# A tuned attention and gated-FFN kernel: the first gate ahead of the sixth pair's outputs, and the attention pieces of one stage a position on

## The chip, the cores and the metric

The kernel runs on one core of a Trainium2 chip. The metric is device time in microseconds of one execution. The engines are TensorE (PE, with its weight loads shown as PEld), VectorE (DVE), ScalarE (ACT), GpSimd (POOL) and SyncE (SP), which issues the DMAs.

## The reference

Sliding-window attention, then a gated FFN on its output, in float32:

```python
scores = scale * np.matmul(q, k.transpose(0, 1, 3, 2))      # 8 batches, 8 heads, 576 x 64
mask = (rel >= 0) & (rel < window)                           # window 64
scores = np.where(mask, scores, -1000000000.0)
scores = scores - np.max(scores, axis=-1, keepdims=True)
attn = np.exp(scores)
attn = attn / (np.sum(attn, axis=-1, keepdims=True) + 1e-09)
x = np.matmul(attn, v)                                       # then laid out as 4608 tokens x 512
gate = 1.0 / (1.0 + np.exp(-(x @ w_gate)))                   # w_gate, w_val: 512 x 1536
val = x @ w_val
return (gate * val @ w_out).astype(np.float32)               # w_out: 1536 x 512
```

The weights come as float64 and are made into float32 on the chip.

## The kernel before, in words

**Tiles.** The 4608 tokens are cut into 12 tiles t of 384. A tile's attention is done in four head pairs p. The suffix of a name tells both: p0_4_0 is head 0 of pair 0 of tile 4. The FFN runs over 12 hidden blocks j of 128. To keep float32 accuracy, each operand of a large product is split into a high and a low part (the names x, w, hh and hl), and each product is three matmuls.

**A head pair's attention** goes through stages. `scores` (L208) is 24 small matmuls into s. `exponentials` masks and takes a row minimum on VectorE (L232), then exps on ScalarE (L241), with row sums rs. `invert` (L249, L250) makes quotients of the sums, and `normalize` (L259) multiplies them in, on VectorE for tiles 4 and 5, on GpSimd for tiles 0 to 2. `stage_b` transposes on TensorE (L290, tile pp) and copies to pT on ScalarE (L295). `stage_c` or `outputs` multiplies with v on TensorE (L319, tile oo), and x (L325 on ScalarE, L326 on VectorE) is the split result.

**The FFN of tiles 0 and 1** is plain. `up_gate` and `up_val` are twelve matmuls each into ph0 and ph1 (L349). The gate is a sigmoid on ScalarE (L372), h32 and its split follow on VectorE (L394, L386, L388), and the down product is y (L419). Exp and sigmoid need different function tables on ScalarE, and a change between them shows as ACT_TABLE_LOAD. The weight conversion of each block (L111 and L112, L145 on ScalarE; L120, L122, L124, L146 on VectorE) runs beside it.

**Tiles 2 to 11** go in five pairs s = 1 to 5, by a scheme of seven products in place of eight. For each k of 0 to 5, products n = 0 to 6 are made for the gate (m = 0) and then for the value (m = 1), in `product` (L568, tile pr). VectorE adds them up: p1, u1, u3, c3, c5, c6 (L574, L580). Gates come behind products 3 to 6 of m = 0. One product of one m is a slot: 14 to a k, 84 to an s. During s the attention of the next two tiles is done between the products; for s = 1 these are tiles 4 and 5. Weight sums for s = 1 are built on GpSimd (L496 to L499) and split into ws, by a cast on ScalarE (L145) and a subtraction on GpSimd (L146).

**The order.** Each piece of work is put into a list with a time and a priority:

```python
def put(tm, o, f, *a):
    events.append((tm, o, f, a))
```

The list is sorted, and each engine gets its instructions in that order, moved a little by a scheduler. So the numbers in the calls of `put` say only the order. For the attention of the first two tiles, n = 0 to 7 counts the eight pairs, with times 3.6 apart and an offset for each stage. The first `up_gate` and `up_val` of tile 0 are put from `now` on. For the pair stages, a dictionary `fill` says which stage is issued behind which slot: number 3 is `stage_s` (scores and exps, with the outputs of the pair before), 4 `stage_n` (quotients), 1 `stage_b` (transposes and copies), 2 `stage_c`.

Of the kernel before, what the change touches and what calls it, by code (L numbers as in the profile page):

```python
# [26 lines left out]
def attn_ffn(ctx: ExitStack, tc: tile.TileContext, qT, kT, vN, w_gate, w_val, w_out, out):  # L27
# [31 lines left out]
    for h in range(2):  # L59
        rows = band[h * BLK:(h + 1) * BLK]  # L60
        nc.gpsimd.affine_select(out=rows, in_=rows, pattern=[[1, P]], compare_op=ALU.is_ge,
                                fill=NEG, base=-1, channel_multiplier=-1)
        nc.gpsimd.affine_select(out=rows, in_=rows, pattern=[[-1, P]], compare_op=ALU.is_ge,
                                fill=NEG, base=BLK, channel_multiplier=1)
    for h, key in enumerate(((1, 0), (0, 1))):
# [3 lines left out]
                                fill=NEG, base=-BLK, channel_multiplier=0)  # L69
# [545 lines left out]
    def hidden_b(s, j):  # L615
        r, k = divmod(j, NK)
        hidden_split(2 * s + 1, j, hb[(s, k)][:, r, :], nc.vector)
# [5 lines left out]
    def put(tm, o, f, *a):  # L623
        events.append((tm, o, f, a))
# [16 lines left out]
    for n in range(2 * NP):  # L641
        t, p = divmod(n, NP)
        for f, d in zip((scores, softmax, stage_b, stage_c),
                        (0, 3.5 if n > 1 else 0, {6: 9.2, 7: 7.3}.get(n, 10.6), {6: 10.4}.get(n, 12.2))):
            put(A0 + 3.6 * n + d, 6, f, t, p)


# [1 line left out]
    def unit(s, n):  # L649
        return 2 * s + n // 2 % 2, n // 4 + n % 2 * 2  # L650

    plan, fill = [], {}
# [7 lines left out]
    at, now = {}, 0.0  # L660
# [5 lines left out]
    def attend(i):  # L666
        nonlocal now
        for f, t, p, *done in fill.get(i, ()):
            if f in (0, 3):
                put(now - LOAD_AHEAD, 8, load_qk, t, p)  # L670
                put(now - LOAD_AHEAD, 8.5, load_v, t, p)
            put(now, 6, stages[f], t, p, *done)
            now += APT[f]

    for i, (kind, t, j) in enumerate(plan):
        attend(i)
        at[(kind, t, j)] = now
        if (kind, t, j) == ("up", 0, 0):
            now = -9
        if kind == "up":  # L680
            put(now, 9, up_gate, t, j)
            now += UPT / 2
            attend(i + 0.5)
            put(now, 9, up_val, t, j)
            if t == 1 and j < NF - KEEP:
                put(now, 9.1, put_hidden, t, j)
            now += UPT / 2
        else:
            for x in range(TB):
                put(now + x * DPT, 9, down, t, j, x, j == 0, j == NF - 1)  # L690
            now += DNT
        if (kind, t, j) == ("up", 0, 0):
            now = 0.0
# [11 lines left out]
    def last_tile(t, js, ready):  # L705


        nonlocal now
        items = [(j, x) for x in range(TB) for j in js[:2]] + [(j, x) for j in js[2:-2] for x in range(TB)]
        items += [(j, x) for x in range(TB) for j in js[-2:]]  # L710
        for n, j in enumerate(js):
            put(now + n * DNT - ready[0], 9.4, ready[1], t, j)
        for n, (j, x) in enumerate(items):
            if n % TB == 0 and t == 1:
                attend(len(plan) + n // TB)
                attend(len(plan) + n // TB + 0.5)
            put(now, 9, down, t, j, x, j == js[0], j == js[-1])
            now += DPT
# [6 lines left out]
    for s in range(1, NS):  # L725
        a, b = 2 * s, 2 * s + 1
        for c in range(2):
            put(now - 21 + 10 * c, 5, x_parts, s, c)
            for n in range(NPR):
                put(now - 19.5 + 10 * c + 1.2 * n, 5.5, x_part, s, n, c)  # L730
                put(now - 18 + 10 * c + 1.2 * n, 5.6, x_rest, s, n, c)
        downs = []
        fill.clear()
        if s + 1 < NS:

            for n, (i, d) in enumerate(((2, 7), (12, 9), (26, 5), (33, 9), (47, 5), (54, 9), (68, 5), (75, 5))):
                fill[i] = [(3, *unit(s + 1, n), *([unit(s + 1, n - 1)] if n else []))]
                fill[i + (2 if n else 4)] = [(4, *unit(s + 1, n))]
                fill[i + d] = [(1, *unit(s + 1, n))]
            fill[82] = [(2, *unit(s + 1, n))]  # L740
        slot = 0
        for k in range(NK):
            if s == 1:
                for m in range(2):
                    for d, f in ((-6, sums_load), (0, sums_make), (7, sums_split), (11, sums_store)):
                        put(now - (21 if k else 38) + 13 * m + d, 7, f, m, k)
                for x, d in enumerate((-18, -14, -5)):
                    put(now + d, 7.5, a_load, s, k, x)
            else:
                for q in range(NPR):  # L750
                    put(now - 24 + 3 * q, 7.5, w_load, s, k, q)
            for m in range(2):
                for n in range(NPR):
                    put(now, 9, product, s, k, m, n)
                    now += PRT
                    if n in (2, 4, 6) and len(downs) > (RESERVE if m else 0) * (k == 1):
                        j, x = downs.pop(0)
                        put(now, 9, down, a, j, x, j == 0, False)
                        now += DPT
                    attend(slot)  # L760
                    slot += 1
            downs += [(j, x) for j in (k, k + NK) for x in range(TB)]
        for j, x in downs:
            put(now, 9, down, a, j, x, False, j == NF - 1)
            now += DPT
        last_tile(b, [n // 2 + (n % 2) * NK for n in range(NF)],
                        (4, lambda t, j, s=s: hidden_b(s, j)))
# [59 lines left out]
```

## Time and profile before

| what | value |
|---|---|
| time, median of 3 runs | 1007.4 us (1005.68 to 1008.06) |
| time of the profiled execution | 1007.45 us |
| its span | 1005.6 us |
| TensorE busy | 978.7 us (97%) |
| VectorE, ScalarE, GpSimd busy | 642.6, 530.7, 232.1 us |
| granted TensorE clock, mean | 0.996 of full |

The span runs from the first to the last instruction that the profiler saw; the time of the run is 1.85 us longer. Busy times are sums over all instructions of an engine. TensorE's weight loads lie beside its matmuls and are counted apart.

### The profile page before, as it was taken

Reading aid. Unit: us, or ns where it says so; the run is one execution under the profiler, and the core shown is the slowest. Engines: PE = TensorE matmul, PEld = TensorE weight load, DVE = VectorE, ACT = ScalarE, POOL = GpSimd, SP = SyncE. Lnnn points to the kernel's source line nnn. Section 1 sums busy time; section 2 is a strip of 40 time slices with the busy share of each in tenths; the row PEclk is TensorE's granted clock in tenths of the full one; section 3 lists DMA queues with packets and bytes.
Section 4 is the critical chain, followed back from the end, with each engine's and each line's share of the span. In section 5 each row is a group of like instructions: output and inputs, shape, how many; then the busy total and the mean of one; then the engine's idle time right before and its main releaser. Section 6 shows DMA issues by size and latency. Waiting matters only on the chain.

```text
span 1005.6 us, 19700 instructions
## 1 busy us (share of the span) xinstructions
PE 978.7 (97%) x6984; PEld 882.5 (88%) x6984; DVE 642.6 (64%) x1737; ACT 530.7 (53%) x1433; POOL 232.1 (23%) x240
## 2 busy tenths in 40 slices
PE   6899999999999999999999999999999999999998
PEld 4788999888888888999988999988999998999996
DVE  7799888636666664666665666565666667344532
ACT  7888887635645745545554554464565464211122
POOL 4210113226453130212131121213211124010100
PEclk9999999999999999999999999999999999999999
DMA  9999988478875624766642676661776652466500
GB/s 298 333 323 361 340 280 273 159 237 291 262 253 195 213 90 166 243 211 222 213 152 86 231 247 199 221 193 42 239 229 218 208 183 72 157 213 206 189 32 32
DMA packets 115057, 208.91 MB, mean 208 GB/s; under 512 B 9360, under 2 KB 61840, under 8 KB 114960
## 3 DMA queue, kind: packets, MB, share of 16 engines
q1 hardware_dynamic: 114960, 207.66, 63.0%
q8 instruction: 56, 0.92, 0.4%
q14 instruction: 41, 0.34, 0.1%
HBM read 165.94 MB, written 41.68 MB: 206 GB/s over the span
## 4 chain that ended last, share of the span: by engine, by line
PE 64%; ACT 4%; DVE 1%; issue 0%; DVEq 0%; ACTq 0%
PE pr L568 35%; PE y L419 23%; PE s L208 2%; ACT p L241 2%; PE pp L290 2%; PE s L319 1%; ACT g L362 1%; ACT e L361 0%; PE pr L319 0%; PE oo L319 0%; DVE u L574 0%; ACT L241 0%; DVE rs L249 0%; DVE c L574 0%; DVE g L366 0%
## 5 line engine op out<-in xcount | busy, mean ns | idle before, releaser
L419 PE MATMUL y<-w,hh 128*128 128x512 f32 x804 | 250.2, 392 | 0.0
L568 PE MATMUL pr<-x_T,wt 128*128 128x384 f32 x1152 | 226.3, 338 | 0.4
L568 PEld LDWEIGHTS pr<-x_T,wt 128*128 128x128 f32 x1152 | 202.2, 188 | 10.9 <-DVE u L574 4.1
L568 PE MATMUL pr<-x_B,wt 128*128 128x384 f32 x864 | 176.4, 340 | 0.1
L419 PEld LDWEIGHTS y<-w,hh 128*128 128x128 f32 x804 | 148.3, 188 | 21.3 <-ACT hh L384 1.3
L419 PE MATMUL y<-w,hl 128*128 128x512 f32 x402 | 158.2, 394 | 0.0
L568 PEld LDWEIGHTS pr<-x_B,wt 128*128 128x128 f32 x864 | 150.5, 188 | 8.2 <-issue 2.6
L574 DVE TENSOR_TENSOR u<-pr,p 128x384 f32<-128x384 f32 x120 | 66.5, 554 | 137.1 <-PE pr L568 136.7
L259 POOL TENSOR_TENSOR p<-p,rs 128x384 f32<-128x384 f32 x76 | 65.8, 880 | 291.1 <-DVE rs L250 212.0
L241 ACT ACTIVATE p<-p,mn 128x128 f32<-128x128 f32 x288 | 111.1, 394 | 23.0 <-DVE mn L232 22.2
L388 POOL TENSOR_TENSOR hl<-h,hh 128x384 fp32r<-128x384 f32 x48 | 49.8, 1039 | 283.4 <-DVE hh L386 283.4
L349 PE MATMUL ph<-x,w 128*128 128x384 f32 x576 | 106.8, 339 | 0.0
L349 PEld LDWEIGHTS ph<-x,w 128*128 128x128 f32 x576 | 100.1, 189 | 2.0 <-issue 1.0
L419 PEld LDWEIGHTS y<-w,hl 128*128 128x128 f32 x402 | 75.3, 187 | 17.8 <-DVE hl L388 1.6
L232 DVE CUSTOM_DVE_ANT_0 p<-s,m 128x128 f32<-128x128 f32 x288 | 66.2, 286 | 14.8 <-PE s L208 14.8
L574 DVE TENSOR_TENSOR c<-pr,u 128x384 f32<-128x384 f32 x120 | 66.7, 555 | 9.9 <-ACT g L372 4.8
L388 DVE TENSOR_TENSOR hl<-hb,hh 128x384 fp32r<-128x384 f32 x60 | 39.1, 663 | 41.1 <-ACT hh L384 40.7
L295 ACT COPY pT<-pp 128x384 f32<-128x384 f32 x96 | 41.7, 482 | 42.9 <-PE pp L290 42.4
L582 ACT COPY p<-pr 128x384 f32<-128x384 f32 x48 | 22.5, 470 | 68.1 <-PE pr L568 67.8
L384 ACT CAST hh<-hb 128x384 fp32r<-128x384 f32 x60 | 30.0, 513 | 51.2 <-PE y L419 51.2
L208 PE MATMUL s<-k,q 64*64 64x128 f32 x1152 | 45.9, 288 | 8.9 <-DMA k<-in_kT_dram 6.9
L574 DVE TENSOR_TENSOR c<-pr,p 128x384 f32<-128x384 f32 x60 | 33.4, 557 | 27.9 <-PE pr L568 27.0
(95 smaller groups left out, 1409.6 us busy)
## 6 DMA issues: line engine op xcount, KB each, us to landing
wt<-wd SPq DMA_DIRECT2D x168, 512.0 KB, 4.0
v<-in_vN_dram SPq DMA_DIRECT2D x48, 384.0 KB, 4.7
wd<-ws SPq DMA_DIRECT2D x48, 256.0 KB, 3.6
k<-in_kT_dram SPq DMA_DIRECT2D x48, 224.0 KB, 4.8
q<-in_qT_dram SPq DMA_DIRECT2D x48, 192.0 KB, 4.6
wd<-w SPq DMA_DIRECT2D x36, 256.0 KB, 5.8
wa<-wd SPq DMA_DIRECT2D x36, 256.0 KB, 4.0
out_dram<-yo SPq DMA_DIRECT2D x33, 256.0 KB, 2.0
```

The costliest lines, as they stand in the source:

```text
L208: pe(nc.tensor.matmul(sc[h][half * BLK:(half + 1) * BLK, u, :], qt[h * BLK:(h + 1) * BLK, U * BLK:(U + 1) * BLK], kt[h * BLK:(h + 1) * BLK ...
L232: nc.vector.tensor_tensor_reduce(out=pt[:, u, :], in0=sc[:, u, :], in1=masks[key], op0=ALU.add, op1=ALU.min, scale=-SCALE, scalar=3.0e38, ...
L241: exp = nc.scalar.activation(pt[:, u, :], pt[:, u, :], AF.Exp, bias=mn[:, u:u + 1], scale=-1.0, **sums)
L259: eng.tensor_mul(out=pt, in0=pt, in1=rs.unsqueeze(2).broadcast_to([P, UP, P]))
L295: cp = nc.scalar.copy(pT, pp)
L349: pe(nc.tensor.matmul(ph, l, r, start=i == 0, stop=i == len(prs) - 1))
L384: nc.scalar.copy(h_hi, h32)
L388: return eng.tensor_sub(out=h_lo, in0=h32, in1=h_hi.bitcast(F32))
L419: pe(nc.tensor.matmul(yb[y], l, r, start=first and n == 0, stop=last and n == 2))
L568: pe(nc.tensor.matmul(ps, l, r, start=new and i == 0, stop=i == len(prs) - 1, skip_group_check=not new))
L574: nc.vector.tensor_add(out=o, in0=ps, in1=a)
L582: nc.scalar.copy(tmp["p1"], ps)
```

## The change

It has two parts. In the head, the transposes of the eighth pair (n = 7) are due one unit earlier, the outputs of the seventh (n = 6) two units later, and the first gate starts at -9.9 in place of -9. In stage s = 1 alone, the scores of the first pair move from slot 2 to slot 5, all quotients go three slots behind their scores (they went two behind, the first four), and the transposes of five of the eight pairs go six slots behind their scores; four of these went five behind before, and the first pair's go from slot 9 to slot 11.

```diff
--- before.py
+++ after.py
@@ -641,7 +641,7 @@
     for n in range(2 * NP):
         t, p = divmod(n, NP)
         for f, d in zip((scores, softmax, stage_b, stage_c),
-                        (0, 3.5 if n > 1 else 0, {6: 9.2, 7: 7.3}.get(n, 10.6), {6: 10.4}.get(n, 12.2))):
+                        (0, 3.5 if n > 1 else 0, {6: 9.2, 7: 6.3}.get(n, 10.6), 12.4 if n == 6 else 12.2)):
             put(A0 + 3.6 * n + d, 6, f, t, p)
 
 
@@ -676,7 +676,7 @@
         attend(i)
         at[(kind, t, j)] = now
         if (kind, t, j) == ("up", 0, 0):
-            now = -9
+            now = -9.9
         if kind == "up":
             put(now, 9, up_gate, t, j)
             now += UPT / 2
@@ -733,9 +733,13 @@
         fill.clear()
         if s + 1 < NS:
 
-            for n, (i, d) in enumerate(((2, 7), (12, 9), (26, 5), (33, 9), (47, 5), (54, 9), (68, 5), (75, 5))):
+
+            slots = ((2, 7), (12, 9), (26, 5), (33, 9), (47, 5), (54, 9), (68, 5), (75, 5))
+            if s == 1:
+                slots = ((5, 6), (12, 9), (26, 6), (33, 9), (47, 6), (54, 9), (68, 6), (75, 6))
+            for n, (i, d) in enumerate(slots):
                 fill[i] = [(3, *unit(s + 1, n), *([unit(s + 1, n - 1)] if n else []))]
-                fill[i + (2 if n else 4)] = [(4, *unit(s + 1, n))]
+                fill[i + (3 if s == 1 else 2 if n else 4)] = [(4, *unit(s + 1, n))]
                 fill[i + d] = [(1, *unit(s + 1, n))]
             fill[82] = [(2, *unit(s + 1, n))]
         slot = 0
```

TensorE in the head, from the transposes of pair 1_1 (pp) to the first gate product of tile 1 (ph0_1_0), before (repeated rows of a group left out):

```order
L290 MATMUL pp1_1_1_686<-ident_105,p1_1_1_566 128x128 x3
L319 MATMUL oo_1_1_716<-pT0_1_1_684,v_1_1_216 64x64
...
L290 MATMUL pp0_1_2_732<-ident_105,p0_1_2_626 128x128 x3
...
L349 MATMUL ph0_0_0_744<-x_0_0_388,w0_0_447 128x384 x3
...
L319 MATMUL oo_1_2_759<-pT0_1_2_736,v_1_2_224 64x64
...
L290 MATMUL pp0_1_3_775<-ident_105,p0_1_3_692 128x128 x3
...
L349 MATMUL ph1_0_0_787<-x_0_0_388,w1_0_592 128x384 x3
...
L319 MATMUL oo_1_3_819<-pT0_1_3_779,v_1_3_226 64x64
...
L349 MATMUL ph0_1_0_835<-x_1_0_677,w0_0_447 128x384 x3
```

And after the change:

```order
L290 MATMUL pp1_1_1_686<-ident_105,p1_1_1_566 128x128 x3
L349 MATMUL ph0_0_0_716<-x_0_0_388,w0_0_447 128x384 x3
...
L319 MATMUL oo_1_1_731<-pT0_1_1_684,v_1_1_216 64x64
...
L290 MATMUL pp0_1_2_747<-ident_105,p0_1_2_626 128x128 x3
...
L290 MATMUL pp0_1_3_759<-ident_105,p0_1_3_692 128x128 x3
...
L349 MATMUL ph1_0_0_771<-x_0_0_388,w1_0_592 128x384 x3
...
L319 MATMUL oo_1_2_790<-pT0_1_2_751,v_1_2_224 64x64
...
L319 MATMUL oo_1_3_819<-pT0_1_3_763,v_1_3_226 64x64
...
L349 MATMUL ph0_1_0_835<-x_1_0_677,w0_0_447 128x384 x3
```

The first gate product ph0_0_0 went from behind the transposes of pair 1_2 to ahead of the outputs of pair 1_1; the transposes of pair 1_3 stand ahead of ph1_0_0's place and the outputs of pair 1_2 behind it.

ScalarE at the first visit of s = 1, from the last copy of the stage ahead to the last gate of m = 0, k = 0 (p is the exp of pair 4_0, ws a weight sum's cast, g a gate), before:

```order
L241 ACTIVATE p0_4_0_3059,rs_4_0_3061<-p0_4_0_3059,mn0_4_0_3060 128x128 x3
L241 ACTIVATE p1_4_0_3068,rs_4_0_3061<-p1_4_0_3068,mn1_4_0_3069 128x128 x3
L145 CAST ws0_0_1_3076<-sw_0_1_2993 128x2x256
L372 ACT_TABLE_LOAD
L372 ACTIVATE g_3_6_3099<-c3_0_1_0_3097 128x384
L372 ACTIVATE g_2_0_3107<-pr0_0_1_0_3017 128x384
L372 ACTIVATE g_2_6_3117<-c5_0_1_0_3115 128x384
L145 CAST ws2_0_1_3079<-sw_0_1_2993 128x2x256
L372 ACTIVATE g_3_0_3127<-c6_0_1_0_3125 128x384
```

And after the change:

```order
L145 CAST ws0_0_1_3065<-sw_0_1_2987 128x2x256
L372 ACT_TABLE_LOAD
L372 ACTIVATE g_3_6_3055<-c3_0_1_0_3053 128x384
L372 ACTIVATE g_2_0_3063<-pr0_0_1_0_3017 128x384
L372 ACTIVATE g_2_6_3086<-c5_0_1_0_3084 128x384
L241 ACT_TABLE_LOAD
L241 ACTIVATE p0_4_0_3102,rs_4_0_3104<-p0_4_0_3102,mn0_4_0_3103 128x128 x3
L241 ACTIVATE p1_4_0_3111,rs_4_0_3104<-p1_4_0_3111,mn1_4_0_3112 128x128 x2
L145 CAST ws2_0_1_3068<-sw_0_1_2987 128x2x256
L241 ACTIVATE p1_4_0_3111,rs_4_0_3104<-p1_4_0_3111,mn1_4_0_3112 128x128
L372 ACT_TABLE_LOAD
```

The six exps stood ahead of the cast and the gates. Now they stand between the third gate and the fourth (g_3_0, which comes right behind the last row), and two table loads are added.

ScalarE at pair 5_0 in s = 1, from the pair's last exps to the last gate of its k (pT are the copies of the transposed weights):

```order
 L241 ACTIVATE p1_5_0_3534,rs_5_0_3526<-p1_5_0_3534,mn1_5_0_3535 128x128 x3
-L295 COPY pT0_5_0_3623<-pp0_5_0_3619 128x384
-L295 COPY pT1_5_0_3629<-pp1_5_0_3625 128x384
+L145 CAST ws0_0_3_3642<-sw_0_3_3566 128x2x256
 L372 ACT_TABLE_LOAD
 L372 ACTIVATE g_3_8_3617<-c3_0_1_2_3615 128x384
-L372 ACTIVATE g_2_2_3637<-pr0_0_1_2_3557 128x384
-L145 CAST ws0_0_3_3642<-sw_0_3_3566 128x2x256
+L372 ACTIVATE g_2_2_3625<-pr0_0_1_2_3557 128x384
+L295 COPY pT0_5_0_3634<-pp0_5_0_3630 128x384
+L295 COPY pT1_5_0_3640<-pp1_5_0_3636 128x384
 L372 ACTIVATE g_2_8_3663<-c5_0_1_2_3661 128x384
```

The two copies went from ahead of the table load to behind the second gate, and the cast of a weight sum the other way. Pair 5_1 has the same move of its copies.

## Rows read from the trace of the kernel before

**Rows 1.** The page, part 1: busy us of each engine, share, instructions.

```profile
PE 978.7 (97%) x6984; PEld 882.5 (88%) x6984; DVE 642.6 (64%) x1737; ACT 530.7 (53%) x1433; POOL 232.1 (23%) x240
```

**Rows 2.** The waits of TensorE: who waits for whom, total us, times, longest.

```profile
PE oo L319 <- ACT pT L295: 4.9, 4, 2.3
...
PE pr L568 <- DVE u L574: 3.6, 6, 0.7
```

**Rows 3.** Timeline of the head: start, us, engine, line, operation [idle before <- releaser].

```profile
29.52 0.53 DVE L326 TENSOR_TENSOR x<-oo,x 128x384 fp32r<-128x384 f32 x1
...
31.32 0.87 PE L290 MATMUL pp<-ident,p 128*128 128x128 f32 x6
...
33.98 0.84 ACT L295 COPY pT<-pp 128x384 f32<-128x384 f32 x2
...
34.50 1.73 PE L319 MATMUL oo<-pT,v 128*64 128x64 f32 x24 [2.31 <-ACT pT L295]
...
36.26 0.48 ACT L325 CAST x<-oo 128x384 fp32r<-128x384 f32 x1 [1.44 <-PE oo L319]
...
39.34 0.62 ACT L145 CAST w<-w 128x512 fp32r<-128x512 f32 x1 [0.72 <-DVE w L124]
...
40.16 0.92 PE L319 MATMUL oo<-pT,v 128*64 128x64 f32 x24
...
41.64 2.33 PE L349 MATMUL ph<-x,w 128*128 128x384 f32 x12
...
44.75 0.96 PE L349 MATMUL ph<-x,w 128*128 128x384 f32 x4
```

**Rows 4.** One window of the head: busy us, then granted clock, DMA share, GB/s.

```profile
35.00:39.00 4.00, 4.00 (x34) 3.88 (x35) 2.10 (x5) 2.37 (x5) 0.83 (x1) 0.57 1.06 394
```

**Rows 5.** Timeline of the first visit of s = 1.

```profile
221.76 0.40 ACT L241 ACTIVATE p<-p,mn 128x128 f32<-128x128 f32 x1 [3.72 <-DVE mn L232]
...
222.48 1.20 PE L568 MATMUL pr<-x_B,wa 128*128 128x384 f32 x6
...
224.71 1.28 ACT L372 ACT_TABLE_LOAD   x1
...
225.23 2.12 DVE L259 TENSOR_TENSOR p<-p,rs 128x384 f32<-128x384 f32 x2
...
225.36 1.58 POOL L146 TENSOR_TENSOR ws<-sw,ws 128x512 fp32r<-128x512 f32 x1
...
226.00 0.52 ACT L372 ACTIVATE g<-c 128x384 f32<-128x384 f32 x1
...
226.96 1.33 PE L568 MATMUL pr<-x_B,wa 128*128 128x384 f32 x6 [1.20 <-ACT g L372]
...
232.97 1.21 PE L568 MATMUL pr<-x_T,wa 128*128 128x384 f32 x6
```

**Rows 6.** Timeline near the second pair's softmax in s = 1 (VectorE).

```profile
274.18 0.97 DVE L249 SCALAR_TENSOR_TENSOR rs<-rs 128x6 f32<-128x6 f32 x1 [1.21 <-ACT p L241]
```

**Rows 7.** Timeline around pair 5_0's transposes, copies and outputs.

```profile
263.90 0.98 PE L290 MATMUL pp<-ident,p 128*128 128x128 f32 x6 [0.70 <-DVE p L259]
...
264.45 0.95 ACT L295 COPY pT<-pp 128x384 f32<-128x384 f32 x2 [2.01 <-PE pp L290]
...
264.72 0.56 DVE L574 TENSOR_TENSOR c<-pr,u 128x384 f32<-128x384 f32 x1
...
267.64 0.69 PE L319 MATMUL s<-pT,v 128*64 128x64 f32 x16
```

**Rows 8.** Timeline: pair 5_1's outputs.

```profile
338.83 0.69 PE L319 MATMUL s<-pT,v 128*64 128x64 f32 x16
```

**Rows 9.** Timeline: first weight-sum product behind the last pair's quotients.

```profile
346.83 1.32 PE L568 MATMUL pr<-x_T,ws 128*128 128x384 f32 x6 [0.49 <-DVE u L574]
```

**Rows 10.** Timeline and a window of the stage behind the head, near 93 us.

```profile
93.49 1.29 PE L319 MATMUL oo<-pT,v 128*64 128x64 f32 x24 [1.00 <-ACT pT L295]
...
90.00:100.00 10.00, 8.95 (x85) 7.61 (x84) 9.97 (x21) 7.06 (x14) 0.00 (x0) 1.00 1.00 348
```

## The prediction

> **What bounds the kernel now.** I read the page's busy shares first. TensorE is at work for 978.7 of 1005.6 us and no other engine reaches two thirds [rows 1], so the sum of the work is TensorE's, and the change neither adds a matmul nor takes one away. What it can move is TensorE's idle time, about 27 us, and the stretches in which TensorE runs at the lower clock. So I read the waits next, TensorE's alone: 4.9 us lie in four waits of attention outputs for the copies of transposed weights, 3.6 us in six waits of products for VectorE's sums u [rows 2]. Then I looked at the stretches that the diff touches: the head, and the product stage of s = 1 (217 to 350 us).
>
> In the head TensorE stands idle for 2.31 us before oo_1_1, because ScalarE brings pT_1_1 only at 33.98 + 0.84 = 34.82 [rows 3]. From 35 to 39 us, right after that idle time, the granted clock is 0.57 on average, so TensorE mostly ran at 1.2 GHz there [rows 4]. The same 24 small matmuls take 1.73 us at that clock and 0.92 us at 2.4 GHz [rows 3].
>
> **The change, part by part.** The sums are made against the profiled execution: span 1005.6 us, 1007.45 us in all (1.85 us outside the span). The three runs before have their median at 1007.4 us, so the profiled one stands for it.
>
> *A. Head.* ph0_0_0 now stands between pp_1_1 and oo_1_1. Its inputs are there (the last half of x_0_3 is written at 29.52 + 0.53 = 30.05), pp_1_1 ends at 32.19, and twelve such matmuls take 2.33 us at full clock [rows 3]. They fill the wait: TensorE is busy until 34.5, and oo_1_1 starts when pT_1_1 is there, at 34.82. With 0.3 us idle in place of 2.31 us I expect no fall of the clock. Then oo_1_1 (0.92), the transposes of two pairs (0.87 each) and ph1_0_0 (2.33) end at 39.8, and oo_1_2 at 40.7. oo_1_3 then has a new wait. ScalarE does the table load (1.28 us [rows 5]) and the first gate (0.5) behind pT_1_1, so x_1_1's cast goes from 36.26 to about 36.6. From that cast to the end of w0_1's cast it takes 39.34 + 0.62 - 36.26 = 3.70 us [rows 3]; one more copy (0.42, half of the 0.84 pair) now stands ahead of that cast, and pT1_1_3 behind it: 36.6 + 3.7 + 0.4 + 0.4 = 41.1. oo_1_3 runs to 42.0, and ph0_1_0 starts there instead of at 44.75 [rows 3]. A = **-2.75**. Bounds: without the wait for pT1_1_3 it would be -3.1; if a later stage takes it back, 0. Queued behind the moved load on ScalarE are x_1_1's cast and w0_1's conversion; their reader, ph0_1_0, comes late enough. SP gets one v load ahead of two weight stores; v_2_0 belongs to tile 2, whose outputs come some stages later, so I cost that at nothing.
>
> *B. First visit of s = 1.* The scores of the first pair (24 small matmuls, which I take at the 0.92 us of the outputs' 24 [rows 3]) move from behind product 2 to behind product 5, so product 4 ends at 222.48 + 1.20 - 0.92 = 222.8 [rows 5]. The cast of a weight sum waits for that product and is now first on ScalarE: from 222.85 to 223.45 (0.6 us, as w0_1's cast [rows 3]), table load to 224.73, two gates (0.5 each) to 225.75. The next product (m = 1) needs the second gate, and TensorE comes to it at 226.96 - 1.20 = 225.76. Its wait of 1.20 us goes, by a hair. What is late next is the softmax: behind the third gate (226.2) ScalarE loads the exp table (1.28) and does six exps and a cast; before, these seven took from 221.76 to the next load at 224.71 [rows 5]. So they end at 226.2 + 1.3 + 2.9 = 230.4. VectorE's scaling, reciprocal and two quotients follow, now behind u1 and ahead of u3. Two quotients would take 2 x 0.56 us, as a sum of that size does [rows 7]; beside GpSimd's work they take longer: they took 2.12 us while GpSimd split a weight sum [rows 5], and the scaling took 0.97 us in the same company [rows 6]. That split follows the cast here too. I take 2.6 us for the four: quotients done at 233.0. TensorE reaches pp_4_0 five products later; from the first product to product 5 it took 232.97 - 226.96 = 6.0 us with the transposes (0.87 [rows 3]) among them, so 225.76 + 5.1 = 230.9, and it waits some 2 us. With the transposes behind that, product 5 of m = 1 starts at 233.85 instead of 232.97 [rows 5]. B = **+0.8** (the lost wait of 1.20 counted in it). Bounds: -1.2, if the quotients are in time; +1.5, if everything is as slow as the slowest rows.
>
> *C. Pair 5_0.* Its transposes move behind product 4 and a piece of the down product, so their wait of 0.70 us goes [rows 7]. But the copies pT_5_0 now stand on ScalarE behind the gate's table load and two gates, and the load waits for VectorE's c, done at 264.72 + 0.56 = 265.28 [rows 7]. So load to 266.56, gates (0.5 each) to 267.5, copies (0.95) to 268.4. The outputs that need them started at 267.64 and start at 268.4. The 0.70 us saved turn into a wait of 1.4. C = **+0.75** (bounds -0.7, if the copies are in time, and +0.8).
>
> *D. Pair 5_1.* Same order, no wait to save. The copies (0.86 to 0.95) go behind the gates, which ended right ahead of the outputs, at 338.83 [rows 8]. D = **+0.8** (bounds 0 and +0.85).
>
> *E. Last pair, 5_3.* u1 goes ahead of the second quotient, so the product that waits 0.49 us for it [rows 9] has it 0.5 us sooner. E = **-0.4** (0 to -0.5). The other five waits for u stay, since at those pairs the quotients stay ahead of u. Pair 4_1's transposes and copies also move, but a product still stands between them and the outputs, and no table load ahead of the copies: nothing.
>
> The two extra table loads are costed inside B, at 1.28 us each by their row: the first gate starts at 226.00, 1.29 us behind the start of its load at 224.71 [rows 5].
>
> The Trainium skill ("ScalarE: Activation LUTs", What ACT_TABLE_LOAD costs) gives some 1.28 us for the load and about 1.38 us more for a drain at each switch. This trace agrees with the first figure (1.28 us) and leaves no room for the second behind the load (1.29 us from start to first gate); by the page, the two extra loads would put some 2.8 us more on ScalarE, and the sum would be about +2.0.
>
> Sum: -2.75 + 0.8 + 0.75 + 0.8 - 0.4 = **-0.8**, so 1007.45 - 0.8 = 1006.6 us.
>
> **The rivals.**
>
> *R1: the moves of s = 1 pay.* The copies of 5_0 and 5_1 are in time and the first quotients come 1.1 us sooner than I think, if product 4 or ScalarE runs ahead of my chain. For it: the waits of 0.70 and 1.20 us do stand there [rows 5, 7]. Against it: the load waits for c in the order after the change. A -2.75, B -0.3, C -0.7, D 0, E -0.4: -4.15, so 1003.3 us.
>
> *R2, slower: the head's gain is given back.* TensorE waits for copies of pT three more times [rows 2]. The longest of these waits is 1.00 us, where the copies stand among the weight conversions on ScalarE, in a stretch where VectorE is busy 9.97 of 10 us and the DMA engines are full [rows 10]. If that pipeline of loads and conversions sets the pace, TensorE comes 2.75 us earlier and waits that much longer there. Then A is 0 and the sum is +1.95: 1009.4 us. It makes the kernel slower as soon as less than 1.95 of the 2.75 us last. Against it: the conversions of the head also start sooner, behind the earlier x_1_3.
>
> *R3: the clock falls all the same.* The short wait for pT_1_1 and that for pT1_1_3 remain. From oo_1_1 to oo_1_2 the half clock costs at least 5.66 - (0.92 + 0.87 + 2.33) = 1.5 us [rows 3]. A would be -1.2, the sum +0.75: 1008.2 us.
>
> *R4: both extra loads stand on the path.* I count one of them in the chain behind which product 5 of m = 1 waits. The second, back to the gates, stands ahead of the copies of pT_4_0 and of the third gate of product 6; if TensorE waits for that too, 1.28 us [rows 5] and what the copies lose behind it (some 0.8, as in D) come on top: the sum is +1.3, 1008.7 us. The page of the Trainium skill named above would make it 1.4 us more per load.
>
> **How the numbers follow.** Chances: the forecast 0.50 (own range 1005.0 to 1008.2, from the bounds of B, C and D with A between -3.1 and -2), R1 0.25, R2 0.14, R3 0.07, R4 0.04. A measurement of this kernel tells about 0.2%, 2.0 us, from no change: faster lies below 1005.4, slower above 1009.4. R1 is faster in five cases of six (0.21), the forecast in one of six (0.08): 0.29, of R3 none. Slower: half of R2 (0.07), a third of R4 (0.01), a tenth of the forecast, since a wait in the head can turn up that no row shows (0.05): 0.13. The rest, 0.58, is no change that can be told. The range runs from 1003.6, which leaves out two fifths of R1 (0.10), to 1008.9, which leaves out most of R2 and some of R4 (0.10).
>
> **What would show it.** Right: no wait between pp_1_1 and ph0_0_0; granted clock 1.00 from 35 to 39 us; ph0_1_0 near 42.0; the wait of 1.20 us at the first product of m = 1 gone and one of some 2 us before pp_4_0; outputs of 5_0 and 5_1 waiting 1.4 and 0.8 us for ScalarE's copies; the wait of 0.49 us gone; two more table loads. Wrong: the waits near 74 and 93 us grown by as much as the head gained (R2); a clock near 0.5 between 33 and 42 us (R3); no wait at the outputs of 5_0 and 5_1 (R1). What I can't see in the rows is whether the exps wait for more than ScalarE, and how GpSimd's split falls beside the quotients: B can be off by 1 us either way.

## The result and the profile after

The changed kernel takes 1009.14 us in the median (1007.71 to 1010.97), the kernel before 1007.19 us beside it (1005.68 to 1008.66). The ratio is 1.0019, with a 95% interval of 1.0012 to 1.0025: about 1.95 us slower, where 1006.6 us, 0.8 us faster, was forecast. It lies just above the range (1008.9). The profiled execution took 1010.81 us (span 1009.0), 1.7 us above its median, so the positions below, which all come from profiled executions, add up to more than the medians differ: 3.4 us in place of 1.95.

The page of the changed kernel, part 1 (busy us of each engine, share, instructions):

```profile
PE 980.6 (97%) x6984; PEld 884.5 (88%) x6984; DVE 641.2 (64%) x1737; ACT 533.7 (53%) x1435; POOL 231.8 (23%) x240
```

The same 6984 matmuls are busy 1.9 us longer than in [rows 1], so somewhere the clock was lower; the rest of the 3.4 us by which the span grew is idle time. ScalarE has its two more table loads. TensorE's waits (for whom, us in total, times, longest):

```profile
PE oo L319 <- ACT pT L295: 5.0, 4, 2.6
PE pr L568 <- DVE u L574: 2.9, 4, 0.7
PE pp L290 <- DVE p L259: 2.6, 3, 1.4
...
PE s L319 <- ACT pT L295: 1.8, 2, 1.3
```

Two of the six waits for u are gone [rows 2]. The wait of outputs for copies in the head stage is as long as before, and there are new waits: transposes for the quotients (the longest 1.4) and the outputs of s = 1 for their copies (1.3 and 0.4).

Where the time went is read best from one kind of work that both kernels have at the same places: the scores of a pair (L208). The table gives the start of five of them in each profiled execution, in us, and between the last three how long the stretch took. 57 and 97 lie in the stage behind the head, 189 ends it, 189 to 235 is the first visit of s = 1, 235 to 432 the rest of that stage and the next.

| kernel | near 57 | near 97 | near 189 | to 235 | to 432 |
|---|---|---|---|---|---|
| before | 57.46 | 97.00 | 189.07 | 45.88 | 197.44 |
| after | 54.91 | 96.94 | 189.02 | 48.27 | 198.26 |
| head alone | 54.95 | 94.89 | 186.99 | 45.85 | 197.47 |
| s = 1 alone | 58.09 | 97.13 | 189.20 | 48.24 | 198.57 |
| first pair alone | 55.99 | 95.21 | 187.25 | 48.23 | 197.47 |
| other pairs alone | 57.40 | 96.78 | 188.88 | 45.85 | 198.46 |
| first pair, filled, copies first | 57.64 | 96.82 | 188.90 | 46.82 | 198.65 |
| u1 ahead at four pairs | 58.56 | 98.51 | 190.57 | 45.87 | 196.44 |
| head, gate late | 55.58 | 97.61 | 188.93 | 45.84 | 197.51 |
| head + u1 ahead at four | 55.38 | 97.65 | 189.70 | 45.87 | 196.39 |

The first two rows tell the story of the change: 2.55 us won at 57 us, none of it left at 97; 48.27 - 45.88 = 2.39 lost in the first visit; 198.26 - 197.44 = 0.82 lost in the rest of s = 1. Behind that, to the end of the span, it loses 0.2 us more. The right two columns repeat to a few hundredths where the kernels have the same edits, with two exceptions: the last is 198.26 and 198.57 with the same edits in s = 1, so a difference of 0.3 us there says nothing, and the kernel with the wait filled is slower there without an edit (below). The left three, the head, scatter by over 1 us between kernels that are the same up to there.

**The head.** Its timeline in the changed kernel (start, us, engine, line, operation, idle before it and what released it), and two windows of it (busy us, granted clock, DMA share, GB/s):

```profile
33.13 2.34 PE L349 MATMUL ph<-x,w 128*128 128x384 f32 x12
...
35.40 0.92 PE L319 MATMUL oo<-pT,v 128*64 128x64 f32 x24
...
41.36 0.91 PE L319 MATMUL oo<-pT,v 128*64 128x64 f32 x22 [0.53 <-ACT pT L295]
...
42.20 0.96 PE L349 MATMUL ph<-x,w 128*128 128x384 f32 x4
```

```profile
30.00:32.00 2.00, 2.00 (x38) 1.67 (x32) 1.95 (x10) 1.06 (x5) 1.22 (x2) 0.50 1.05 397
...
35.00:39.00 4.00, 4.00 (x47) 3.68 (x46) 1.23 (x3) 3.44 (x6) 0.83 (x1) 1.00 1.04 395
```

ph0_0_0 fills the place of the 2.31 us wait (it starts at 33.13, where 32.19 was forecast), oo_1_1 takes 0.92 where it took 1.73 [rows 3], the clock from 35 to 39 us is 1.00 where it was 0.57 [rows 4], and ph0_1_0 starts at 42.20 (42.0 was forecast). The half clock is not absent from the head; in this execution it came earlier, from 30 to 32 us, where the kernel before had 1.00. Then, farther on:

```profile
54.91 0.89 PE L208 MATMUL s<-k,q 64*64 64x128 f32 x24
...
74.33 1.30 PE L319 MATMUL oo<-pT,v 128*64 128x64 f32 x24 [2.56 <-ACT pT L295]
...
93.40 1.29 PE L319 MATMUL oo<-pT,v 128*64 128x64 f32 x24 [1.31 <-ACT pT L295]
...
96.94 0.89 PE L208 MATMUL s<-k,q 64*64 64x128 f32 x24
```

TensorE waits 1.31 us where it waited 1.00 [rows 10], and 2.56 us at 74.33, where the timeline of before has:

```profile
74.76 1.29 PE L319 MATMUL oo<-pT,v 128*64 128x64 f32 x24 [0.93 <-ACT pT L295]
```

**The first visit of s = 1**, by the timeline of the changed kernel:

```profile
225.55 1.31 PE L568 MATMUL pr<-x_B,wa 128*128 128x384 f32 x6
...
230.19 1.28 ACT L372 ACT_TABLE_LOAD   x1
230.21 0.96 DVE L249 SCALAR_TENSOR_TENSOR rs<-rs 128x6 f32<-128x6 f32 x1 [1.70 <-ACT p L241]
...
231.43 1.81 DVE L259 TENSOR_TENSOR p<-p,rs 128x384 f32<-128x384 f32 x2
231.49 0.52 ACT L372 ACTIVATE g<-c 128x384 f32<-128x384 f32 x1
...
232.39 0.52 PE L290 MATMUL pp<-ident,p 128*128 128x128 f32 x3 [1.36 <-DVE p L259]
...
233.39 0.52 PE L290 MATMUL pp<-ident,p 128*128 128x128 f32 x3 [0.48 <-DVE p L259]
...
233.76 2.12 PE L568 MATMUL pr<-x_T,wa 128*128 128x384 f32 x6
...
235.81 1.12 PE L319 MATMUL s<-pT,v 128*64 128x64 f32 x16
...
237.29 0.92 PE L208 MATMUL s<-k,q 64*64 64x128 f32 x24
```

The first product of m = 1 has no wait; it had 1.20 us [rows 5]. The transposes wait 1.36 + 0.48 = 1.84 us for the quotients. Product 5 of m = 1 then takes 2.12 us for the six matmuls that took 1.21, and the windows say why:

```profile
232.00:234.00 2.00, 1.13 (x7) 0.86 (x8) 1.97 (x4) 0.55 (x3) 1.83 (x2) 1.00 1.02 353
234.00:236.00 2.00, 2.00 (x10) 1.56 (x11) 1.31 (x4) 0.98 (x3) 0.00 (x0) 0.50 1.05 397
236.00:238.00 2.00, 2.00 (x48) 1.85 (x46) 1.97 (x3) 0.85 (x2) 1.34 (x1) 0.65 0.28 106
```

The granted clock is 0.50 from 234 to 236 us and 0.65 from 236 to 238; in the kernel before it is 1.00 throughout 230 to 240, and the next scores start at 234.95:

```profile
230.00:240.00 10.00, 9.92 (x97) 9.08 (x96) 7.63 (x23) 5.13 (x13) 6.15 (x7) 1.00 0.95 296
...
234.95 0.89 PE L208 MATMUL s<-k,q 64*64 64x128 f32 x24
```

**Pairs 5_0 and 5_1:** the outputs now wait for ScalarE's copies, 1.33 and 0.43 us, and the last pair's product has no wait any more [rows 9].

```profile
269.53 0.85 ACT L295 COPY pT<-pp 128x384 f32<-128x384 f32 x2
...
270.05 1.00 PE L319 MATMUL s<-pT,v 128*64 128x64 f32 x15 [1.33 <-ACT pT L295]
...
341.88 1.00 PE L319 MATMUL s<-pT,v 128*64 128x64 f32 x15 [0.43 <-ACT pT L295]
```

### The profile page after: what moved, and what is told of

Same layout as the page of the kernel before. It is cut to its first block, busy times and chain, and to the rows that moved or that the text cites. A ratio compares the mean times of both kernels' runs of the same rounds, so it can differ in the third digit from the quotient of the medians.

```text
span 1009.0 us, 19709 instructions
## 1 busy us (share of the span) xinstructions
PE 980.6 (97%) x6984; PEld 884.5 (88%) x6984; DVE 641.2 (64%) x1737; ACT 533.7 (53%) x1435; POOL 231.8 (23%) x240
## 4 chain that ended last, share of the span: by engine, by line
PE 63%; ACT 4%; DVE 1%; issue 1%; DVEq 0%; ACTq 0%
PE pr L568 35%; PE y L419 23%; PE s L208 2%; ACT p L241 2%; PE pp L290 2%; PE s L319 1%; ACT g L362 1%; ACT e L361 1%; PE pr L319 0%; DVE u L574 0%; PE oo L319 0%; DVE c L574 0%; DVE g L366 0%; ACT e L363 0%; DVE rs L249 0%
## 5 line engine op out<-in xcount | busy, mean ns | idle before, releaser
L208 PE MATMUL s<-k,q 64*64 64x128 f32 x1152 | 46.9, 293 | 8.5 <-DMA k<-in_kT_dram 6.8
```

The lines of the kernel that those rows point to most:

```text
L208: pe(nc.tensor.matmul(sc[h][half * BLK:(half + 1) * BLK, u, :], qt[h * BLK:(h + 1) * BLK, U * BLK:(U + 1) * BLK], kt[h * BLK:(h + 1) * BLK ...
```

## The experiments

Each ratio is against the kernel before, timed beside it. Diffs are against the changed kernel where nothing else is said.

**Head alone.** The table of slots goes back to that of before.

```diff
-            slots = ((2, 7), (12, 9), (26, 5), (33, 9), (47, 5), (54, 9), (68, 5), (75, 5))
-            if s == 1:
-                slots = ((5, 6), (12, 9), (26, 6), (33, 9), (47, 6), (54, 9), (68, 6), (75, 6))
-            for n, (i, d) in enumerate(slots):
+            for n, (i, d) in enumerate(((2, 7), (12, 9), (26, 5), (33, 9), (47, 5), (54, 9), (68, 5), (75, 5))):
...
-                fill[i + (3 if s == 1 else 2 if n else 4)] = [(4, *unit(s + 1, n))]
+                fill[i + (2 if n else 4)] = [(4, *unit(s + 1, n))]
```

> Only the head's part of the change; s = 1 as before. Theory T1 (the profile after: the head's lead of 2.6 us at 57 us is down to 0.06 us at 97 us, because weight conversions and their DMAs set the pace there): no change, within 0.5 us of before, with the wait near 74 us grown from 0.93 to some 2.5 us. Rival T2 (the head's gain lasts, and s = 1 costs so much more): 2 to 2.8 us faster. Rival T3 (the head itself is slower, through a fall of the clock at another place): 1 us or more slower.

Measured: 1006.2 us, ratio 0.9993 (0.9984 to 1.0001). Its profiled execution has these scores:

```profile
54.95 0.89 PE L208 MATMUL s<-k,q 64*64 64x128 f32 x24
...
94.89 0.89 PE L208 MATMUL s<-k,q 64*64 64x128 f32 x24
...
430.31 0.89 PE L208 MATMUL s<-k,q 64*64 64x128 f32 x24
```

This one execution keeps 2.1 of its 2.5 us, but the times do not: over eleven executions the head is worth some 0.7 us (0.07% of 1006.75), and the interval takes in nothing and 1.6 us. A profile of one execution is too little to judge the head by.

**s = 1 alone.** The head's two edits go back.

```diff
-                        (0, 3.5 if n > 1 else 0, {6: 9.2, 7: 6.3}.get(n, 10.6), 12.4 if n == 6 else 12.2)):
+                        (0, 3.5 if n > 1 else 0, {6: 9.2, 7: 7.3}.get(n, 10.6), {6: 10.4}.get(n, 12.2))):
...
-            now = -9.9
+            now = -9
```

> Only the part of the change in stage s = 1; the head as before. T1: the whole loss is here, 2 to 3.2 us slower (first visit 2.3, pair 5_0 0.7, pair 5_1 0.8, last pair -0.3, the rest -0.3). T2: some 4.5 us slower. T3: 1 us or less.

Measured: 1010.12 us, ratio 1.0035 (1.0022 to 1.0047), 3.4 us slower. The same waits stand at the same places (1.35 and 0.48 us before the transposes at 232.55 and 233.55), and the clock is 0.83 from 230 to 240 as in the changed kernel. The whole loss, and more, is in s = 1.

**First pair alone**, of the edits in s = 1 (against the kernel before; in the four other rows of slots nothing moves).

```diff
+            slots = ((2, 7), (12, 9), (26, 5), (33, 9), (47, 5), (54, 9), (68, 5), (75, 5))
+            if s == 1:
+                slots = ((5, 6), (12, 9), (26, 5), (33, 9), (47, 5), (54, 9), (68, 5), (75, 5))
...
-                fill[i + (2 if n else 4)] = [(4, *unit(s + 1, n))]
+                fill[i + ((2 if n else 3) if s == 1 else 2 if n else 4)] = [(4, *unit(s + 1, n))]
```

> In s = 1 only the first visit moves (scores from slot 2 to slot 5, its quotients and transposes behind it); all else as before. T1: 2.3 us slower in the profile, of which some 0.8 are the wait at the transposes of pair 4_0 and 1.5 are a stretch of 2 to 3 us at a granted clock of 0.5 right behind that wait. Rival T4 (the fall of the clock is an accident of the one execution): 0.8 us slower, clock 1.00 behind the wait.

Measured: 1010.44 us, ratio 1.0035 (1.0021 to 1.0048). Its trace, with a window over the place:

```profile
230.60 0.52 PE L290 MATMUL pp<-ident,p 128*128 128x128 f32 x3 [1.36 <-DVE p L259]
231.60 0.80 PE L290 MATMUL pp<-ident,p 128*128 128x128 f32 x3 [0.48 <-DVE p L259]
232.05 2.27 PE L568 MATMUL pr<-x_T,wa 128*128 128x384 f32 x6
```

```profile
232.00:234.00 2.00, 2.00 (x8) 1.81 (x6) 1.45 (x3) 0.99 (x2) 0.05 (x1) 0.50 1.03 364
234.00:236.00 2.00, 2.00 (x45) 1.69 (x48) 1.61 (x3) 0.89 (x2) 0.91 (x1) 0.72 0.28 109
```

The first visit takes 48.23 - 45.88 = 2.35 us more and the rest of s = 1 nothing more (197.47 against 197.44). So the first pair alone brings the whole of B, and the half clock comes again behind the same two waits. Its time is 3.5 us longer, more than these 2.35: from 432 us to the end of the span it loses another 0.7 us, at places near 615 and 850 us that the edit doesn't touch. The two kernels with the wait filled, below, lose 0.7 and 0.9 us there as well, the whole of the change 0.2, s = 1 alone nothing; the cause stays open.

**Other pairs alone.** The first pair's slots go back, the others stay; the head's two edits go back too, as with s = 1 alone.

```diff
-                slots = ((5, 6), (12, 9), (26, 6), (33, 9), (47, 6), (54, 9), (68, 6), (75, 6))
+                slots = ((2, 7), (12, 9), (26, 6), (33, 9), (47, 6), (54, 9), (68, 6), (75, 6))
...
-                fill[i + (3 if s == 1 else 2 if n else 4)] = [(4, *unit(s + 1, n))]
+                fill[i + ((3 if n else 4) if s == 1 else 2 if n else 4)] = [(4, *unit(s + 1, n))]
```

> In s = 1 the first visit as before; only the other pairs' quotients and transposes a slot on. T1: 1.0 to 1.3 us slower: outputs of 5_0 and 5_1 wait 1.3 and 0.4 us or more for ScalarE's copies, the wait of 0.70 us at 5_0's transposes is gone, the last pair gains 0.3. Rival (copies are in time without the first visit's delay): 1 us faster.

Measured: 1008.55 us, ratio 1.0017 (1.0008 to 1.0026). The first visit takes as long as before (45.85 us), the rest 198.46 - 197.44 = 1.02 us more; the outputs of 5_0 wait 1.33 us at 267.71. In the traces the two parts add up to s = 1 alone: 2.35 + 1.02 = 3.37, against 2.36 + 1.13 = 3.49. The times don't, 3.5 and 1.7 against 3.4; the 0.7 us behind 432 are part of that, and the intervals are wide.

**First pair, with the wait filled.** Is the half clock the second half of B, or is it the order? Twelve transposes of the identity, work that no one needs, stand ahead of pair 4_0's real ones, so that TensorE is busy through the wait (against the kernel with the first pair alone).

```diff
             pp = bank(t, p, f"p{h}", f"pp{h}_{t}_{p}")
+            if (t, p) == (4, 0):
+                for u in range((9, 3)[h]):
+                    pe(nc.tensor.transpose(pp[:, u % UP, :], ident, ident))
             for u in range(UP):
```

> As the run that moves only the first visit, with twelve more transposes of the identity ahead of pair 4_0's own (nine and three, into the same tiles, overwritten at once): they do nothing but keep TensorE busy while it would wait for the quotients. T1 (the wait makes the clock fall, and the fall costs more than the wait): granted clock 1.00 from 230 to 240 us, product 5 of m = 1 no later than without the filling, its six matmuls 1.2 us instead of 2.1; 1.5 us faster than the first visit alone, 0.8 to 1 us slower than before. T4 (the clock falls there for another reason): as slow as the first visit alone, 2.3 us or more.

Measured: 1011.26 us, ratio 1.0033 (1.0021 to 1.0046), no better. The clock did stay up (1.00 from 230 to 240, product 5 in 1.33 us), but in the order that came out ScalarE casts the hidden values (hh) ahead of both copies of pT_4_0, and the outputs waited 0.65 us for them at 235.92; more was lost behind 340 us. By itself that settles nothing; the next kernel puts the copies first again.

**First pair, filled, copies first.** The cast is issued behind the copies.

```diff
+        if (t, p) == (4, 0):
+            with tc.issue_after(cp.ins):
+                tmp.pop("late")()
...
-            hidden_split(t, j, h32, t_engine(s))
+            if (t, j) == (2, 0):
+                tmp["late"] = lambda: hidden_split(t, j, h32, t_engine(s))
+            else:
+                hidden_split(t, j, h32, t_engine(s))
```

> The filled first visit again, with the copies of pT_4_0 kept ahead of the cast hh_2_0 on ScalarE, as they stand without the filling (the first filling put the cast ahead, and the outputs of 4_0 waited 0.65 us for the copies). T1: granted clock 1.00 from 230 to 240 us, no wait of the outputs, the scores of pair 4_2 some 0.9 us later than before instead of 2.34: 1.4 us faster than the first visit alone. Rival (a price of the new place that is no clock and no wait): still 2 us or more later.

Measured: 1010.77 us, ratio 1.0031 (1.0019 to 1.0043). Its trace at the place, and the window:

```profile
233.63 1.31 PE L574 MATMUL pr<-x_T,wa 128*128 128x384 f32 x6
234.88 0.69 PE L325 MATMUL s<-pT,v 128*64 128x64 f32 x16
...
235.72 0.89 PE L208 MATMUL s<-k,q 64*64 64x128 f32 x24
```

```profile
234.00:236.00 2.00, 2.00 (x40) 1.68 (x41) 1.89 (x5) 1.48 (x4) 0.51 (x1) 1.00 0.99 356
```

Clock 1.00, product 5 in 1.31 and the outputs in 0.69 us as before the change, and the first visit takes 46.82 - 45.88 = 0.94 us more in place of 2.35. So the clock costs 1.4 us of B, and the order 0.9, close to the 0.8 that was forecast for B. The total shows nothing of it: behind 235 us this kernel loses 198.65 - 197.44 = 1.21 us, with a down product that waits 0.40 us for VectorE at 372.69. There every engine has its instructions in the same order as before. GpSimd's sums (t), which the casts and VectorE's subtractions (x_T) there wait for, start at 364.01 us, while with the first pair alone they start at 362.55, with TensorE at the same place: GpSimd waits for the store of an output tile, which takes 3.4 us from its issue to its landing in place of 2.0. Why it does is open. Another 0.9 us goes behind 432. The split of B is shown at its place, not in the time of the kernel.

**Quotients behind u1 at every pair of s = 1** (against the kernel before: the quotients of all but the first pair go three slots behind the scores, and the order puts those of all pairs behind u1).

```diff
     def stage_n(t, p):
-        invert(sums_of[(t, p)])
-        for h in range(2):
-            normalize(t, p, h)
+        with tc.issue_after(marks["u"]) if t in (4, 5) and marks.get("u") else nullcontext():
+            invert(sums_of[(t, p)])
+            for h in range(2):
+                normalize(t, p, h)
...
+            marks["u"] = last_add[0]
```

> The kernel before, with one edit in s = 1: the quotients of the pairs stand behind u1 of the same product block on VectorE (an order that five of the eight pairs do not have before). My step E in full: the five waits of 0.5 to 0.7 us of products for u1 go, 3.4 us; the quotients come 0.6 us later. If the transposes can bear that: 2.5 to 3.4 us faster. Rival (the wait moves on to the transposes, as the first visit's did): within 1 us of before, with 3 or 4 new waits of some 0.5 us at transposes.

Measured: 1007.36 us, ratio 0.9997 (0.9987 to 1.0007): no change that can be told. The five waits of 0.5 to 0.7 us for u went, and others came in their place, six at transposes for the quotients (4.0 us in all, where two had 1.5) and one for u at another product; the longest two of them:

```profile
286.77 1.34 PE L571 MATMUL pr<-x_T,ws 128*128 128x384 f32 x6 [0.74 <-DVE u L577]
...
348.55 0.99 PE L291 MATMUL pp<-ident,p 128*128 128x128 f32 x6 [1.56 <-DVE p L259]
```

TensorE had won 1.1 us by 339 us and lost 1.2 us at the last pair, whose transposes come too soon behind the late quotients. A wait for u is moved, not removed, unless the transposes go later too.

**Quotients behind u1 at four pairs** (4_1, 4_3, 5_1, 5_3; in the table, u1 ahead at four pairs). Their quotients go three slots behind their scores, and the transposes of 4_1 and 5_3 one slot later than before (against the kernel before; u1 is marked as in the last diff).

```diff
+        with tc.issue_after(marks["u"]) if (t, p) in ((4, 1), (4, 3), (5, 1), (5, 3)) else nullcontext():
...
-            for n, (i, d) in enumerate(((2, 7), (12, 9), (26, 5), (33, 9), (47, 5), (54, 9), (68, 5), (75, 5))):
+            for n, (i, d) in enumerate(((2, 7), (12, 9), (26, 5), (33, 9), (47, 6 if s == 1 else 5), (54, 9), (68, 5), (75, 6 if s == 1 else 5))):
...
-                fill[i + (2 if n else 4)] = [(4, *unit(s + 1, n))]
+                fill[i + ((3 if s == 1 and n > 3 else 2) if n else 4)] = [(4, *unit(s + 1, n))]
```

> The kernel before with u1 ahead of the quotients at pairs 4_1, 4_3, 5_1 and 5_3, and the transposes of 4_1 and 5_3 behind product 4, as the change has them, so that they do not wait for the later quotients. My term E at four places: 0.7 + 0.7 + 0.5 + 0.4, 2.3 us faster. Rival (the waits move on, as they did at all five places together): no change.

Measured: 1006.27 us, ratio 0.9988 (0.998 to 0.9996). That is about 1.2 us faster, where 2.3 was expected. The rest of s = 1 takes 197.44 - 196.44 = 1.0 us less; 0.7 us of what the pairs save is given back at the last one, whose outputs now wait:

```profile
351.60 1.29 PE L320 MATMUL oo<-pT,v 128*64 128x64 f32 x24 [0.66 <-ACT pT L296]
```

**A fourth buffer for the converted weights, without and with the head.** ScalarE waits for stores of w32d in the stage behind the head (below), so the pool of w32 gets four buffers in place of three; e has to give one of its two.

```diff
-    RAW, W32 = 6, 3
+    RAW, W32 = 6, 4
...
-        e = mp.tile([P, TT], F32, name=f"e_{nm}", tag="e", bufs=2)
+        e = mp.tile([P, TT], F32, name=f"e_{nm}", tag="e", bufs=1)
```

> The kernel before with a fourth buffer for the converted weights (and one less for e, used from tile 4 on). What paces the weight conversion behind the head: T5, the loop conversion, store, buffer free: ScalarE's waits for the stores w32d (2.4 us in 36 to 100 us) go, and the lead of TensorE at 97 us over the kernel before is 0.5 to 1.5 us. Rival T6, the DMA engines' throughput: nothing changes at 97 us (within 0.3 us).

> The head's part of the change with the fourth buffer. T5: the lead of 2.5 us at 57 us lasts to 97 us and to the end, 2.5 us or more faster than before. T6: the lead at 97 us is somewhere between 0 and 2 us, as without the buffer, and the time is that of the head's part alone.

Measured: 1026.23 us, ratio 1.019 (1.0176 to 1.0204), and 1028.14 us, ratio 1.0202 (1.0187 to 1.0216). The single buffer of e makes both far slower, but only from 390 us on, as in the first of them:

```profile
393.59 1.34 PE L568 MATMUL pr<-x_B,wt 128*128 128x384 f32 x6 [2.17 <-ACT g L362]
```

So only the part ahead of 100 us says something on the head. There the scores start at 55.78 and 96.46 without the head's edits, at 55.02 and 95.94 with them, 40.7 and 40.9 us apart. The waits for stores are 3.0 us in all in both. The kernel with head and fourth buffer stood 2.44 us ahead of the kernel before at 57 us and 1.06 at 97, and 0.76 and 0.52 us ahead of its own counterpart without the head's edits. With one execution of each, and starts that scatter by over 1 us, this doesn't show whether the buffer keeps the lead; the waits for stores it did not remove.

**Head, with the gate late.** The gate products stay early on TensorE, but ScalarE does the table load and the first gate two units later, behind w0_1's cast and the copies (against the head alone).

```diff
+    held = {}
+
+    def up_first(t, j):
+        held[0] = up(t, j, 0)
+
+    def gate_first(t, j):
+        gate_table(t, j, held.pop(0))
...
-            put(now, 9, up_gate, t, j)
+            if (kind, t, j) == ("up", 0, 0):
+                put(now, 9, up_first, t, j)
+                put(now + 2.0, 9, gate_first, t, j)
+            else:
+                put(now, 9, up_gate, t, j)
```

> The head's part of the change with the matmuls of the first gate where the change puts them, but ScalarE's table load and gate behind the cast of w0_1 and the copies of pT_1_3. H2 (what eats the head's lead is the table load ahead of the conversion of w0_1, which delays that store by 1 us and leaves the DMA engines short of work from 37 to 45 us): the store of w32_0_1 some 2 us sooner than with the change, lead at 97 us of 2 us or more, 2 us faster than before. H1 (the pace of conversions and stores behind the head eats it whatever stands here): as the head's part alone, 0.3 to 1 us faster.

Measured: 1006.4 us, ratio 0.9992 (0.9984 to 1.0001), the same as the head alone. 1.9 us ahead at 57 us, 0.6 us behind at 97, with a wait of 2.19 us in between:

```profile
74.27 1.92 PE L319 MATMUL oo<-pT,v 128*64 128x64 f32 x24 [2.19 <-ACT pT L295]
```

The lead is gone without the early load and gate on ScalarE too, in this execution and by the times, so they are not what takes it.

**Head and quotients behind u1 at four pairs**: the head's edits of the change, and the four pairs with their quotients behind u1 in place of the change's s = 1.

> The head's part of the change and u1 ahead of the quotients at the four pairs: the two parts that the runs show as gains. 2.3 us of s = 1 and 0.5 to 1.4 of the head: 2.8 to 3.7 us faster than before. If the waits move on: 0.5 to 1.4 us.

Measured: 1005.46 us, ratio 0.9981 (0.9972 to 0.999), about 1.9 us faster than before (2.8 to 3.7 was expected) and the best of all; by the two ratios it is 3.8 us below the changed kernel. Its trace again has the lead at 57 us (55.38) gone at 97 (97.65); the rest of s = 1 takes 196.39 us, 1.05 less than before.

## Why the prediction was wrong

**A, the head (-2.75 forecast): the step failed, by the rival R2.** The steps up to 42 us came as worked out, and TensorE was 2.55 us ahead at 57 us. What failed is the last step, that the lead stays. The waits at 74.33 and 93.40 grew from 0.93 and 1.00 to 2.56 and 1.31, and with a few tenths more nothing was left at 97. This is more than one execution's chance: over the eight profiled executions with the old head (those of the table, that with the wait filled, 57.99 and 97.14, and that with u1 ahead at every pair, 58.76 and 97.68; the fourth buffers left out) the scores start at 57.74 and 97.03 in the mean; over the four with the new head, the late gate among them, at 55.21 and 96.77. The lead falls from 2.5 to 0.3 us on average; only the head alone kept 2.1 of it. By the times the head is worth 0.7 us alone, 0.8 with the gate late, 0.7 on top of the four pairs (0.9988 to 0.9981), 1.6 on top of s = 1 (1.0035 to 1.0019). I take it for about 1 us; the intervals leave about 1 us either way.

TensorE gives it back in its waits for ScalarE's copies, which stand among the conversions of the weights, as R2 had it: near 74 us these waits are 0.2 to 1.1 us in the eight kernels and 1.3 to 2.6 in the four. From 60 to 80 us VectorE is busy for 19.43 of 20 us before and 19.52 after, so it has hardly any idle time to give up when TensorE is early (the windows of before and after; VectorE is the third sum):

```profile
60.00:80.00 20.00, 19.02 (x143) 17.51 (x142) 19.43 (x50) 17.94 (x39) 2.52 (x2) 1.00 0.99 332
...
60.00:80.00 20.00, 17.35 (x131) 15.22 (x130) 19.52 (x53) 16.96 (x37) 1.99 (x2) 1.00 0.94 326
```

ScalarE's waits in 36 to 100 us show the lead too, first before and then after:

```profile
ACT w L111 <- DMA w32d<-w: 2.4, 2, 1.8
```

```profile
ACT w L111 <- DMA w32d<-w: 7.1, 4, 2.6
```

The kernels with the old head and three buffers have 2.4 to 3.1 us here, those with the new one 3.4 to 7.1. That the copies of pT come hardly sooner when TensorE is early is shown: with 2.55 us of lead the outputs start at 74.33 in place of 74.76. Which link sets the pace, VectorE's work, the stores that free the weight buffers, or the full DMA queues, is not: the runs with a fourth buffer don't tell, and a lighter VectorE was not tried.

**B, the first visit (+0.8): order right, clock missed.** The wait of 1.20 us went, TensorE came to the transposes at 232.39 - 1.36 = 231.03 (230.9 forecast), the quotients were done at 233.24 (233.0), the two waits are 1.84 us (some 2), and product 5 started at 233.76 (233.85): 0.79 us late, as worked out. The sum stopped there. From that product to the next scores it is 237.29 - 233.76 = 3.53 us where it was 234.95 - 232.97 = 1.98, 1.55 us more, because the clock halves behind the waits. With the wait filled this second part goes (0.94 left of 2.35). The prediction had such a row in the head [rows 4] and priced it there, in A and R3, but took the new wait of B at its length alone. Together B is +2.39. The Trainium skill ("TensorE: Matmul & The Clock Gate", HAM oscillation) tells of a kernel whose waits for DMAs between bursts of matmuls bring the low clock back, and of paying for this each time. The loss here is of that kind, with 0.50 and 0.65 behind 1.84 us of waiting; but the waits on that page are longer, so it doesn't say whether ones as short as these lower the clock, and here the trace decides.

**C, pair 5_0 (+0.75), D, pair 5_1 (+0.8), E, last pair (-0.4): right.** Between the scores on either side the changed kernel loses 0.71 and 0.83 us at the two pairs and wins 0.31 at the last. The parts differ a little: the outputs of 5_0 start only 270.05 - 267.64 - 2.07 = 0.34 us later (2.07 is the lag that TensorE brought along), and the block of outputs takes 0.37 us longer in both pairs, because the second copy is late as well; so at 5_1 the wait is 0.43 us, not 0.8, and the rest lies in the block. Two gains of 0.27 and 0.24 us between these places were in no term; they bring the rest of s = 1 to 0.82.

**The rivals.** R2's mechanism came true, and its forecast, 1009.4 us, lies 0.3 us from the median, but partly by chance: it had s = 1 at +1.95 where it is about +3.4, and the head at nothing where it is worth some 1 us. By the times the two parts add up: 3.4 (s = 1 alone) less 0.7 (head alone) is 2.7 us, and 1.95 was measured, within what the intervals leave. R1 is refuted: 5_0 and 5_1 do wait. R3 is refuted where it was put (1.00 from 35 to 39 us). R4 is refuted: the load at 230.19 is done when the gate starts at 231.49, while TensorE waits for VectorE. The gate starts 1.30 us behind the start of its load. The drain that the Trainium skill adds to a load ("ScalarE: Activation LUTs", What ACT_TABLE_LOAD costs) does not show here either; that the sum by that page, +2.0, meets the measured 1.95 is chance, since the loss came from the clock and the head.

**The chances.** Slower by over 0.2% had 0.13; 1.0019 lies just within 0.2%, at its edge. R2 got 0.14 though the profile spoke for it in three rows: the stage behind the head had TensorE waiting for the same copies, with VectorE full [rows 10].

## What to carry to other kernels

A lead won at one place is worth what the next waits leave of it: before counting it, follow the same engine to the next wait, and ask whether the engine that is waited for has any idle time to come sooner; if the work behind that wait keeps an engine busy for 97% of the stretch, don't count on the lead: here, by the times, about 1 of 2.75 us was left, and which link held it back is not shown. Price a new wait of TensorE at more than its length: the matmuls behind it may run at the lower clock, here 1.4 us on top of 1.84, where other work in the wait avoids it. And weigh a place whose start scatters by 1 us between executions by many times, not by one profile.

## What the runs showed of the hardware that was not expected

Not every wait lowered the clock. Behind 1.36 + 0.48 us at the first visit it fell to 0.50 for some 2 us in the changed kernel, with s = 1 alone (234 to 236 us) and with the first pair alone. Behind the wait of 2.56 us at 74.33 in the changed kernel it stayed at 1.00, while behind the wait of 2.19 us at the same place in the kernel with the gate late it fell to 0.50:

```profile
75.00:76.00 1.00, 1.00 (x22) 1.00 (x18) 1.00 (x4) 1.00 (x4) 0.00 (x0) 0.50 0.98 307
```

The single waits of 1.33 us (270.05) and 1.56 us (348.55) left it at 1.00. What decides is more than the length of the wait, and the runs don't settle it; in the head the half clock came at 22 to 24 and 35 to 39 us before, at 30 to 32 us after. Another surprise was how far a small edit reaches: twelve idle transposes at 231 us were followed by 1.2 us lost over 100 us later, where every engine has its instructions in the same order, behind output stores that took 3.4 us to land in place of 2.0.
